# Another table of engine, order, slot and planned time for the 1478 steps of a linear-attention and maxout kernel

## Chip, core and metric

The kernel runs on one NeuronCore of one Trainium2 chip. The metric is device time in microseconds (us) of one launch; a launch takes all inputs from HBM and writes the whole output back to HBM.

## What is computed

The reference is a linear attention with a softmax-like feature map, followed by a maxout feed-forward layer. Its core, shortened:

```python
def phi(x):                                   # q or k: [8, 8, 576, 64], w_phi: [64, 128]
    proj = einsum('bhsd,df->bhsf', x, w_phi)
    proj = proj - max(abs(proj), axis=-1, keepdims=True)
    return concatenate([exp(proj), exp(-proj)], axis=-1)
q_p, k_p = phi(q), phi(k)
kv  = einsum('bhsf,bhsd->bhfd', k_p, v)
num = einsum('bhsf,bhfd->bhsd', q_p, kv)
den = einsum('bhsf,bhf->bhs', q_p, k_p.sum(axis=2))[..., None] + 1e-06
x   = (num / den) with heads side by side     # 4608 tokens x 512
h   = maximum(maximum(x @ w1, x @ w2), x @ w3)  # 768 wide
out = h @ w_out                               # 4608 x 512, float32
```

## The kernel before

**Attention.** The 64 pairs of batch and head are cut into 16 units of four heads (`attention(u)`). Each unit has 18 tiles of 128 rows. A unit goes through these steps, and the letters are the kinds in the code:

- L and Lv load q, k and v. Unit 0 loads q and k in halves as float32 through SyncE's queue (L437) and casts them on VectorE or ScalarE (L444). Units 1 to 3 load q and k through GpSimd's queue with a cast on the way (L451). The later units load float32 through SyncE (L462) and cast on GpSimd (L468). All v loads are SyncE's.
- T transposes q and k, so that the head dimension lies on partitions: on TensorE for units 0 to 3 (L482, with a copy out of PSUM on VectorE at L485), by a transposing DMA on SyncE's queue for the others (L497).
- G projects: for four tiles (or two), one product for q into the bank `psq` and one for k into `psk` (L520). Both have 64 rows of weights, so they use one half of the array's rows each. A unit has five G steps, four of eight products and one of four. Each of them is followed by two reductions of the maximum on VectorE (r, L539) and two exponentials on ScalarE (L533).
- R and V exist from unit 2 on. The q maxima are transposed on TensorE (L547), copied out (mT, L551) and written by a small DMA into a row of the transposed q (V, L555), so that M can subtract the maximum inside the product. Units 0 and 1 subtract it with extra products instead (L601, L604).
- M forms the q projection once more in transposed shape (`psm`, L599), and two exponentials follow on ScalarE (L612).
- v is scaled on GpSimd or VectorE (va, L574), vd fills in the denominator's column (L584), K sums k features times v over 18 tiles (`kvps`, 72 products with 64 rows, L628), N forms numerator and denominator (`psn`, L646), VectorE divides (L652, L653), and X transposes the result into `xT` (on TensorE at L666 for units 0 and 1, by a DMA at L676 for the others).

**Feed-forward.** Nine chunks of 512 tokens (`chunk`) follow the units: eight of one batch each, and one of the 64 last tokens of every batch. w1 was subtracted from w2 and w3 beforehand and w1 @ w_out was formed (L783 transposes w1, L797 multiplies, `pm`). A chunk has 12 up steps of four 128x512 products (`ups`, L699), evacuated by VectorE or ScalarE, and four down tiles: a straight step (L726) and a step over the hidden layer (L731) in one bank `ops`, an evacuation (L739) and a store (L746).

**What sets the order.** Every step is a Node with its engine, its function and its buffers. The string `PLAN` (L96 on) names them in the order in which they are written into the program: the number of the node, the engine (T, D, A, G, S for TensorE, VectorE, ScalarE, GpSimd and SyncE), the slot of each buffer that the step is the first to use, and after the @ a planned time. `plan()` reads it. An engine runs its steps strictly in that order; a step waits for its inputs and for the last users of its slots. The eight PSUM banks are one pool. The planned times only decide one thing more: `fill()` puts idle products (`idler`, L828) into gaps of TensorE's planned times, mostly at the start, so that TensorE keeps running. SyncE, GpSimd and ScalarE also issue DMAs, in the same order as their other steps.

Of the kernel before, what the change touches and what calls it, by code (L numbers as in the profile page):

```python
# [96 lines left out]
0G@0.7 4A@0.7 6S0@0.7 10S0@1.1 2D7@1.1 86G1@1.2 3D@1.5 8S@1.5 13S@2.0 85G@2.0 361S1@2.4 15S0@2.8 1076G@2.9 159G0@3.6 7D2@3.7  # L97
5D@4.2 1G@4.5 158G@5.0 12D@5.1 1079G@5.8 16T5@5.8 17D2@6.5 27T015110@7.3 22T04@7.5 29A@7.8 30D@7.8 28A@8.3 14D@8.6 9A@8.8
26D@9.1 20T5@9.6 31D@9.7 18T6@9.7 24A@9.8 21D@10.3 228G2@10.5 19D@10.5 42T12@10.6 44A@11.0 32T56@11.3 11G@11.3 46D@11.4
1077G@11.4 33A@11.7 35D@11.7 43A@12.2 45D@12.3 23A@12.5 87D3@12.7 25D@12.8 37T31@12.8 88S@12.9 47A1@12.9 93T5@13.0 38A@13.3  # L100
40D@13.4 39A@13.9 94D0@13.9 58T41@14.1 50A0@14.3 41D@14.4 34A@14.5 89T3@14.6 59A@15.0 36D@15.1 55T2@15.2 90D@15.7 61T0@15.8
51A@15.8 60A@16.0 91T3@16.4 63A@16.5 48G@16.9 49D@16.9 67T4@16.9 56A@17.0 64T1@17.3 62A@17.5 68A@17.9 364G1@18.0 115T110601@18.1
69A@18.3 119D@18.5 54A@18.6 66A@18.7 118D@18.8 92D@19.1 53G@19.1 1086T0@19.3 65A@19.3 95T35@19.9 1087A1@20.0 105T71@20.1
52G@20.3 108D@20.6 116A@20.9 109D@21.2 117A@21.3 100T70@21.3 227G@21.4 102A@21.8 103D@21.8 1078G@22.2 57A@22.3 98D@22.4
110T76@22.5 97A@22.8 113D@23.0 162T2@23.1 106A@23.2 101A@23.7 137T30@23.8 163D2@23.8 96A@24.2 166T7@24.2 114D@24.4 164T4@24.5
139A@24.7 1090T2@25.0 167D@25.0 124A1@25.2 165D@25.3 138A@25.4 1088T7@25.5 126G1@25.6 1091A@25.9 70T043@26.0 1089D@26.2
125G@26.7 111A@26.8 140T2@27.2 107A@27.3 104D@27.4 1096T7@27.8 127G@27.8 141A@27.8 72D@28.0 142A@28.2 99D@28.3 112A@28.4
71D@28.9 173T003010@29.1 1097A@29.3 183T56@29.4 73T10@29.6 176D@29.7 174A@29.8 75T4@30.0 187D@30.2 120A@30.3 1094T3@30.4
175A@30.5 121G@30.7 186D@30.8 184A@31.0 160D0@31.4 177D@31.5 185A@31.6 161S@31.7 134T7@31.7 122G@31.8 74D1@32.1 362S1@32.1
79T5@32.2 135A@32.4 128T2@32.5 426S0@32.6 76D0@32.8 1095A@32.9 131T1@33.0 129A@33.4 77T0@33.5 297S0@33.5 80D0@33.5 178T43@33.8  # L110
136A@33.9 1082G@34.0 1098T6@34.1 229D1@34.2 181D@34.3 133A@34.4 182D@34.9 132A@34.9 123A@35.4 168T74@35.5 78D0@35.5 130A@35.6
143T015@35.8 170A@36.1 1080G@36.1 1099D@36.2 180A@36.5 172D@36.8 188T60@36.9 144A@37.2 192D@37.4 145A@37.4 231T2@37.6 191D@37.7
190A@37.8 1092T1@38.1 196A1@38.1 169A@38.3 232D0@38.3 198G0@38.4 189A@38.8 171D@38.9 148T51@39.5 1093A@39.7 152T4@39.8
149D1@40.0 83T0@40.1 199A@40.2 179A@40.4 146T6@40.4 197G@40.5 153D0@40.6 235T2@40.7 84A@40.8 150T1@40.9 236D@41.3 81T5@41.4
147D0@41.5 233T3@41.7 82A@41.9 151D1@42.1 193T6@42.3 154T2@42.4 365G@42.6 194A1@42.7 234D@42.7 242T104701@42.7 155A@43.0
237T10@43.1 195S@43.1 156T6@43.3 245D@43.3 238A@43.6 215T135@43.7 1081G@43.7 296S1@43.8 157D@43.9 243A@44.1 366S1@44.2 241D@44.4
252T24@44.9 246D@45.0 1104T6@45.1 217A@45.1 216A@45.4 255D@45.6 239A@45.7 1112T3@46.1 253A@46.2 240D@46.2 1105A0@46.6 1083D@46.8
247T10@46.9 254A@47.1 257T62@47.3 1110T5@47.4 250D@47.5 1085G@47.8 260D@48.1 203T11@48.4 251D@48.4 1102T6@48.6 1111A@48.6
230S@48.7 256D@49.0 249A@49.1 557S1@49.1 1116T5@49.4 1103A@49.7 1084D@49.9 363S2@50.1 244A@50.2 1114T6@50.3 1117D@50.6 248A@50.7
429G2@50.8 204A@51.1 261D@51.2 209T7@51.2 1124T4@51.4 1113D@51.5 259A@51.6 265A1@51.9 299G0@52.0 258A@52.1 1115D@52.1 262T0@52.3  # L120
1122T5@52.3 205A@52.4 263D0@52.7 210A@52.8 1125D@52.9 264S@53.1 300G@53.1 212T1@53.2 1108T6@53.3 211A@53.4 1123D@53.5 214A@53.9
200T2@54.2 213A@54.3 266G0@54.3 427S0@54.3 367T013010@54.4 1109D@54.4 201A@54.6 387T57@54.7 621S0@54.8 382T14@54.8 371D@55.0
1120T6@55.2 202A@55.2 556S1@55.2 391D@55.6 384A@55.7 385D@55.9 1106T2@56.0 388A@56.2 267G@56.4 383A@56.4 390D@56.5 1121D@56.9
1118T1@56.9 389A@56.9 369A@57.2 370D@57.5 1107A@57.6 377T56@57.8 206T7@58.1 386D@58.1 368A@58.1 1130T2@58.4 208A@58.6 301S2@58.6
380D@58.7 430G@59.1 379A@59.1 224T31@59.3 1119D@59.3 218T0@59.6 207A@59.6 281T50@59.9 225D1@59.9 269T4@60.0 268G@60.2 1131T@60.2
282A@60.2 1101G@60.5 271A@60.5 219D0@60.5 283A@61.0 381D@61.1 270A@61.2 372T57@61.5 624G1@61.7 1132A0@61.8 284T010@61.8
375D@62.1 298S0@62.3 374A@62.4 278T3@62.9 373A@62.9 286D@63.2 220T2@63.2 378A@63.4 376D@63.5 392T4@63.5 1126T0@63.7 279A@63.9
393D1@64.1 221D0@64.3 395A1@64.4 394S@64.5 272T7@64.5 285A@64.6 275T5@64.7 222T4@65.0 273A@65.0 428S3@65.2 287T60@65.3 276A@65.5
# [731 lines left out]
```

## Time and profile before

| | us |
|---|---|
| median of 3 runs (288.76 to 289.62) | 288.84 |
| span of the profiled execution | 287.6 |
| TensorE busy | 275.5 (96%) |
| VectorE, ScalarE, GpSimd busy | 205.7, 198.6, 117.1 |
| idle products (36), busy | 12.0 |
| last product ends | 284.1 |

The span runs from the first to the last instruction of the program; the measured time has 1.2 us more around it. Busy time of TensorE needs care: a record of a 128x512 product is 379 ns long, while the next one starts 216 ns after it, so that records overlap and hide pauses of less than 0.16 us. Starts of successive products are what counts below. Queue times (SPq) are waits of an issuing queue and no work.

### The profile page before, as it was taken

How to read it: one execution, taken by the hardware profiler on the slowest of the kernel's cores; microseconds unless marked ns; L12 is line 12 of the kernel's file. 1: busy time of each engine (PE TensorE's matmuls, PEld its weight loads, DVE VectorE, ACT ScalarE, POOL GpSimd, SP SyncE). 2: the span in 40 equal slices, each digit the busy share in tenths (PEclk: the TensorE clock that was granted, in tenths of full speed). 3: DMA queues.
4: the chain of work that ended last, by engine and by line, in shares of the span. 5: the costliest groups of instructions: out<-in, count | busy, mean ns of one | idle time of the engine just before them, and what ended most of it. 6: DMA issues, size and time to landing. Idle time of an engine off the chain costs nothing.

```text
span 287.6 us, 8596 instructions
## 1 busy us (share of the span) xinstructions
PE 275.5 (96%) x3550; PEld 154.7 (54%) x3590; DVE 205.7 (71%) x434; ACT 198.6 (69%) x460; POOL 117.1 (41%) x100
## 2 busy tenths in 40 slices
PE   8889999999989899999999999999999999999995
PEld 3366675466555455655555466565544654444443
DVE  4679899988979788887879778987863551516511
ACT  1599998999998789895798979997756631040010
POOL 8264688868454349706365434050083000000000
PEclk9999999999999999999999999999999999999999
DMA  7999977999999998999899769787510019410054
GB/s 181 277 248 209 228 298 121 330 282 235 237 176 336 210 260 182 265 267 253 198 238 211 207 122 203 235 171 132 119 41 0 2 41 199 115 34 0 0 153 141
DMA packets 68337, 51.45 MB, mean 179 GB/s; under 512 B 48778, under 2 KB 53066, under 8 KB 68298
## 3 DMA queue, kind: packets, MB, share of 16 engines
q1 hardware_dynamic: 63903, 45.62, 65.6%
q0 software_dynamic: 4000, 4.92, 9.9%
q8 instruction: 28, 0.46, 0.7%
q10 hardware_dynamic: 395, 0.37, 0.4%
q14 instruction: 11, 0.09, 0.1%
HBM read 34.64 MB, written 9.44 MB: 153 GB/s over the span
## 4 chain that ended last, share of the span: by engine, by line
PE 87%; DMA 5%; DVE 3%; ACT 2%; issue 1%; SPq 0%; ACTq 0%; DVEq 0%
PE ups L699 31%; PE ops L731 16%; PE ops L726 10%; PE psn L646 7%; PE kvps L628 6%; PE psq L520 6%; PE psm L599 5%; DMA k_raw<-in_k_dram 3%; DMA qkT<-mT 2%; PE pm L797 2%; DVE mk L539 1%; PE tps L482 1%; DVE mqp L539 1%; ACT Ek L533 1%; ACT Eq L612 1%
## 5 line engine op out<-in xcount | busy, mean ns | idle before, releaser
L699 PE MATMUL ups<-xT,w_bf 128*128 128x512 bf16 x417 | 100.6, 379 | 0.8
L533 ACT ACTIVATE Ek<-psk 128x512 bf16<-128x512 f32 (+1 forms) x160 | 82.0, 572 | 15.3 <-PE psk L520 11.9
L574 POOL TENSOR_TENSOR vab<-v_raw,em 128x1152 bf16<-128x1152 f32 (+1 forms) x35 | 66.8, 1926 | 56.0 <-ACT em L570 45.9
L612 ACT ACTIVATE Eq<-psm 128x512 bf16<-128x512 f32 (+1 forms) x160 | 80.1, 577 | 10.4 <-PE psm L599 9.8
L699 PEld LDWEIGHTS <-w_bf 128*128 128x128 bf16 x432 | 40.2, 98 | 44.4
L539 DVE TENSOR_REDUCE mqp<-psq 128x4 bf16<-128x512 f32 (+1 forms) x80 | 48.5, 633 | 6.4 <-PE psk L520 4.7
L539 DVE TENSOR_REDUCE mk<-psk 128x4 f32<-128x512 f32 (+1 forms) x80 | 49.1, 630 | 5.0 <-PE psk L520 3.3
L731 PE MATMUL ops<-wout_bf,hT 128*128 128x512 bf16 (+2 forms) x219 | 49.8, 367 | 0.6 <-issue 0.3
L705 DVE TENSOR_TENSOR hT<-hT,ups 128x512 bf16<-128x512 bf16 x54 | 35.5, 681 | 16.8 <-PE ups L699 16.3
L739 ACT COPY osb<-ops 128x512 f32<-128x512 f32 (+2 forms) x18 | 10.0, 563 | 36.5 <-PE ops L731 28.9
L707 ACT ACTIVATE hT<-ups 128x512 bf16<-128x512 f32 x38 | 22.4, 612 | 15.5 <-PE ups L699 14.0
L731 PEld LDWEIGHTS <-hT 128*128 128x128 bf16 x228 | 21.1, 98 | 22.2
L653 DVE TENSOR_TENSOR x_sb<-psn,rden 128x320 bf16<-128x320 f32 x64 | 31.5, 492 | 2.2
L646 PEld LDWEIGHTS <-Eq 128*128 128x128 bf16 x640 | 25.9, 98 | 9.7
L739 DVE COPY osb<-ops 128x512 f32<-128x512 f32 (+1 forms) x20 | 13.4, 668 | 21.8 <-PE ops L731 21.6
L646 PE MATMUL psn<-kv_sb,Eq 128*128 128x65 bf16 x640 | 28.2, 194 | 0.0
L520 PE MATMUL psq<-w,qkT 64*128 64x128 bf16 x288 | 24.6, 217 | 2.2 <-DVE mk L539 0.8
L520 PEld LDWEIGHTS <-qkT 64*128 64x128 bf16 x576 | 16.8, 94 | 15.9 <-issue 11.9
L520 PE MATMUL psk<-w,qkT 64*128 64x128 bf16 x288 | 24.5, 217 | 0.2 <-DVE v_raw L460 0.2
L726 PE MATMUL ops<-xT 128*128 128x512 bf16 x85 | 23.1, 379 | 0.9 <-issue 0.5
L599 PE MATMUL psm<-qkT,wphi_m 128*128 128x512 bf16 (+1 forms) x70 | 22.1, 358 | 1.3 <-DMA qkT<-mT 1.2
L652 DVE RECIPROCAL rden<-psn 128x5 f32<-128x5 f32 x64 | 12.1, 189 | 11.8 <-PE psn L646 11.2
(74 smaller groups left out, 237.2 us busy)
## 6 DMA issues: line engine op xcount, KB each, us to landing
v_raw<-in_v_dram SPq DMA_DIRECT2D x16, 576.0 KB
out_dram<-osb SPq DMA_DIRECT2D x65, 128.0 KB
q_raw<-in_q_dram SPq DMA_DIRECT2D x12, 576.0 KB
k_raw<-in_k_dram SPq DMA_DIRECT2D x12, 576.0 KB
w_bf<-in_moe_w_dram POOLq DMA_DIRECT2D x3, 768.0 KB, 15.5
qk_bf<-in_k_dram POOLq DMA_DIRECT2D x3, 288.0 KB, 16.5
qk_bf<-in_q_dram POOLq DMA_DIRECT2D x3, 288.0 KB, 11.6
wout_bf<-in_moe_w_out_dram POOLq DMA_DIRECT2D x1, 768.0 KB, 20.7
```

Source lines behind the costliest of these rows:

```text
L520: nc.tensor.matmul(ps()[:, i, :], lhsT=cols[r, :], rhs=w2[r, c, :], start=True, stop=True)
L533: nc.scalar.activation(Ek[s]()[:, tiles_of(t0, n), :], of(1), EXP, scale=1.0 - 2.0 * s)
L539: nc.vector.tensor_reduce((mq, mk)[c]()[:, tiles_of(t0, n)], of(c), AXX, ALU.max, apply_absolute_value=True)
L574: (nc.vector if n_.eng == "DVE" else nc.gpsimd).tensor_tensor(vab()[:, g, t0:t1, 0:D], vb()[:, t0:t1, :], em()[:, g, t0:t1].unsqueeze(2).t ...
L599: nc.tensor.matmul(psm()[:, 0:w], lhsT=wphi_m, rhs=rhs, start=True, stop=True)
L612: nc.scalar.activation(Eqb()[s][:, cols], psm()[:, 0:w], EXP, scale=1.0 - 2.0 * s)
L646: nc.tensor.matmul(psn()[:, c, :], lhsT=Eqb()[g][:, t0:t0 + P], rhs=kv()[:, pr, ab, g, :], start=(g == 0), stop=(g == 1))
L653: nc.vector.tensor_tensor(x_sb()[:, pr, :, ab, :], psn()[:, :, 0:D], rden().to_broadcast([P, 5, D]), ALU.mult)
L699: nc.tensor.matmul(ups(), lhsT=w_bf[i + 1][:, ct, j * P:(j + 1) * P], rhs=tokens_of(ct), start=(ct == 0), stop=(ct == CT - 1))
L705: nc.vector.tensor_tensor(hT()[:, j, :], hT()[:, j, :], ups(), ALU.max)
L726: nc.tensor.matmul(ops_()[:, 0:width], lhsT=tile_of(ct, tt), rhs=line_w[c_i > MOVE][:, ct, cols], start=(ct == 0), stop=False)
L731: nc.tensor.matmul(ops_()[:, 0:width], lhsT=hT()[:, j, tt * P:(tt + 1) * P], rhs=wout_bf[:, j, cols], start=False, stop=(j == JT - 1))
```

## The change

The program's functions are untouched: the number of every matmul, reduction, exponential and transfer stays. Only the string `PLAN` is another, and it has 13 lines more, so that every line number after it grows by 13 (the products of G are L520 before and L533 now). Its first lines:

```diff
-0G@0.7 4A@0.7 6S0@0.7 10S0@1.1 2D7@1.1 86G1@1.2 3D@1.5 8S@1.5 13S@2.0 85G@2.0 361S1@2.4 15S0@2.8 1076G@2.9 159G0@3.6 7D2@3.7
+2D0@0.70 4A@0.70 10S0@0.70 3D@0.90 6S0@1.18 8S@1.66 13S@2.14 15S0@2.62 11G@3.72 12A0@3.72 0G@3.87 1G@4.42 7D@4.79 86G1@4.92
```

95 of the 1478 steps change their engine (mostly evacuations, between ScalarE and VectorE), and nearly all change their place. All 461 steps of TensorE remain, with 21 idle products where 36 were.

**GpSimd at the start of the program.** Before, the identity was built first and the loads of unit 1 (`qk_bf`), the weights and unit 2 were issued at once:

```order
masks.py:197 MEMSET ident 128x128
masks.py:199 ISA
masks.py:199 AFFINE_SELECT ident<-ident 128x128
L451 DMA qk_bf<-in_k_dram 128x2x576
L451 DMA qk_bf<-in_q_dram 128x2x576
L409 DMA w_bf<-in_moe_w_dram 128x4x768
L451 DMA qk_bf<-in_k_dram 128x2x576
L399 TENSOR_SCALAR minus<-ident 128x128
L451 DMA qk_bf<-in_q_dram 128x2x576
L409 DMA wout_bf<-in_moe_w_out_dram 128x6x512
L451 DMA qk_bf<-in_k_dram 128x2x576
L441 COPY gated<-k_raw 1x1
```

Now the copy `gated`, which waits for the first half of unit 0's k, stands ahead of them all:

```order
L454 COPY gated<-k_raw 1x1
masks.py:197 MEMSET ident 128x128
masks.py:199 ISA
masks.py:199 AFFINE_SELECT ident<-ident 128x128
L412 TENSOR_SCALAR minus<-ident 128x128
L464 DMA qk_bf<-in_k_dram 128x2x576
L464 DMA qk_bf<-in_q_dram 128x2x576
L422 DMA w_bf<-in_moe_w_dram 128x4x768
L464 DMA qk_bf<-in_q_dram 128x2x576
L464 DMA qk_bf<-in_k_dram 128x2x576
L422 DMA wout_bf<-in_moe_w_out_dram 128x6x512
L464 DMA qk_bf<-in_k_dram 128x2x576
```

So GpSimd's first load is issued only after a part of unit 0's data has landed; the two loads of unit 3 come one after the other now, and the weights w2 follow. On SyncE's queue k's first half goes ahead of q's, and the q load of unit 5, which stood ahead of unit 0's v, goes behind unit 1's v.

**TensorE in the last unit's projections.** The names carry buffer numbers here. Before, the G steps of unit 15 follow on one another; this is the end of one (`psk_4764`) and the beginning of the next (`psq_4774`):

```order
L520 LDWEIGHTS qkT_4348
L520 MATMUL psq_4762<-w2_73,qkT_4348 128x128
L520 LDWEIGHTS qkT_4348
L520 MATMUL psk_4764<-w2_73,qkT_4348 128x128
L520 LDWEIGHTS qkT_4348
L520 MATMUL psq_4774<-w2_73,qkT_4348 128x128
L520 LDWEIGHTS qkT_4348
L520 MATMUL psk_4776<-w2_73,qkT_4348 128x128
```

Now the same step of unit 15 ends in front of a down tile's products, which use all 128 rows:

```order
L533 LDWEIGHTS qkT_4578
L533 MATMUL psq_4822<-w2_73,qkT_4578 128x128
L533 LDWEIGHTS qkT_4578
L533 MATMUL psk_4824<-w2_73,qkT_4578 128x128
L739 LDWEIGHTS xT_85
L739 MATMUL ops_4833<-xT_85 128x512
```

This is the rule for all units. G and K have 64 rows of weights in use per product; the transposes of q and k have 128x64; every other product has 128x128. Counted along TensorE's order with idle products left out, the shape of the array's use changes 93 times before and 165 times now. The G and K steps stood in 40 stretches before (9 of a single step, 31 of two to four) and stand in 78 now (62 of a single step, 14 of two, 2 of three).

**VectorE at the same place.** Before, the eight large reductions of unit 15 (`mqp`, `mk`) were a block:

```order
L539 TENSOR_REDUCE mqp0_79<-psq_4762 128x4
L539 TENSOR_REDUCE mqp0_79<-psq_4784 128x4
L539 TENSOR_REDUCE mqp0_79<-psq_4795 128x4
L539 TENSOR_REDUCE mk_4631<-psk_4786 128x4
L539 TENSOR_REDUCE mqp0_79<-psq_4774 128x4
L539 TENSOR_REDUCE mk_4631<-psk_4776 128x4
L539 TENSOR_REDUCE mk_4631<-psk_4764 128x4
L539 TENSOR_REDUCE mk_4631<-psk_4797 128x4
```

Now they are spread among the maxima of the chunk's hidden layer (`hT`) and the divisions:

```order
L552 TENSOR_REDUCE mqp1_80<-psq_4656 128x4
L718 TENSOR_TENSOR hT_4594<-hT_4594,ups_4634 128x512
L718 TENSOR_TENSOR hT_4594<-hT_4594,ups_4683 128x512
L718 TENSOR_TENSOR hT_4594<-hT_4594,ups_4669 128x512
L718 TENSOR_TENSOR hT_4594<-hT_4594,ups_4696 128x512
L665 RECIPROCAL rden_4741<-psn_4723 128x5
L666 TENSOR_TENSOR x_sb_4743<-psn_4723,rden_4741 128x5x64
L552 TENSOR_REDUCE mqp1_80<-psq_4713 128x4
L665 RECIPROCAL rden_4778<-psn_4760 128x5
L666 TENSOR_TENSOR x_sb_4743<-psn_4760,rden_4778 128x5x64
L552 TENSOR_REDUCE mk_4793<-psk_4715 128x4
```

The evacuations of one projection no longer come in a burst; a bank is given back after one or two other steps instead of after up to seven reductions.

Two more moves are spoken of below. The first K of unit 0 stands behind 28 TensorE steps before and behind 25 now: one transposing step of four products (unit 2), one G step of four (unit 1) and one M step (unit 1) that stood ahead of it stand behind it. And in several units fewer TensorE steps lie between R and the first M, which is the time that the copy mT and the small DMA V have. For unit 3 these were 15 steps (six up steps, one straight step, three M, three G and two N of other units); now they are seven (one M, one N, two G, and three steps of down tiles).

More of the change, by code (lines that the diff above doesn't have):

```diff
@@ L101 @@
[L101 to L126, printed above, removed]
```

257 lines of the change are left out of this document (148 added, 109 removed).

## The prediction

> **What bounds the kernel now.** I read the page first (busy shares, chain), then TensorE in four stages, its waits, and single starts in the timeline. From the page:
>
> ```profile
> span 287.6 us, 8596 instructions
> PE 275.5 (96%) x3550; PEld 154.7 (54%) x3590; DVE 205.7 (71%) x434; ACT 198.6 (69%) x460; POOL 117.1 (41%) x100
> PE 87%; DMA 5%; DVE 3%; ACT 2%; issue 1%; SPq 0%; ACTq 0%; DVEq 0%
> GB/s 181 277 248 209 228 298 121 330 282 235 237 176 336 210 260 182 265 267 253 198 238 211 207 122 203 235 171 132 119 41 0 2 41 199 115 34 0 0 153 141
> ```
>
> TensorE holds 87% of the chain that ended last. Where it is not fully busy shows in the stages (window, its length, then PE, PEld, DVE, ACT and POOL busy) and in TensorE's waits (sum, times, longest):
>
> ```profile
> 0.00:27.10 27.10, 23.26 (x289) 12.69 (x290) 18.70 (x45) 17.24 (x41) 13.89 (x23) 1.00 1.04 230
> 27.10:82.00 54.90, 54.27 (x932) 33.12 (x943) 49.74 (x108) 52.32 (x124) 39.96 (x30) 1.00 1.02 242
> 82.00:96.00 14.00, 11.92 (x186) 6.81 (x181) 12.49 (x27) 11.63 (x28) 7.74 (x6) 1.00 0.97 247
> 96.00:284.10 188.10, 186.02 (x2159) 102.05 (x2185) 124.72 (x256) 117.13 (x269) 55.55 (x43) 1.00 0.64 149
> ...
> PE psm L599 <- DMA qkT<-mT: 1.2, 1, 1.2
> ...
> PE psq L520 <- DVE mk L539: 0.8, 1, 0.8
> ```
>
> After 27 us TensorE pauses only between 82 and 96 us. The first stage looks 86% busy, but idle products fill it. So I count TensorE's time from what products cost back to back. Pieces of the chain (start, length) give the rates:
>
> ```profile
> 24.31 0.57 PE tps L482 x16
> ...
> 27.11 1.50 PE kvps L628 x72
> ...
> 36.85 1.09 PE kvps L628 x72
> ...
> 40.02 0.63 PE psn L646 x20
> ...
> 49.05 2.59 PE ups L699 x12
> ...
> 281.46 2.63 PE ops L731 x24
> ```
>
> A 128x512 product takes 2.59/12 = 0.216. The program has 870 of them (432 up, 350 down, 64 M, 24 `pm`): 187.7 us. 16 K at 1.09 make 17.4, 64 N at 0.63/2 20.0. The 80 G steps make 16.1 by the pair steps of 0.056 below (64 of 0.224, 16 of 0.112). The remainder (12 transposing steps, narrow products of M and of the last tile, extra products of units 0 and 1) makes 13.3 at like rates. **Work: 254.5 us.** It doesn't change. The last product ends at 281.46 + 2.63 = 284.1, so 29.6 us are something else.
>
> A part of these is the price of changing the array's shape:
>
> ```profile
> 90.04 1.89 PE L699 MATMUL ups<-xT,w_bf 128*128 128x512 bf16 x8
> 91.86 0.23 PE L520 MATMUL psq<-w,qkT 64*128 64x128 bf16 x1
> ...
> 92.04 0.22 PE L520 MATMUL psk<-w,qkT 64*128 64x128 bf16 x1
> 92.09 0.22 PE L520 MATMUL psq<-w,qkT 64*128 64x128 bf16 x1
> ...
> 92.49 0.22 PE L520 MATMUL psk<-w,qkT 64*128 64x128 bf16 x1
> 92.64 1.04 PE L699 MATMUL ups<-xT,w_bf 128*128 128x512 bf16 x4
> 93.51 1.03 PE L726 MATMUL ops<-xT 128*128 128x512 bf16 x4
> ```
>
> From `ups` to `ops`, same shape, four products take 93.51 - 92.64 = 0.87 = 4 x 0.216. From 90.04 to the first `psq` eight take 1.82, 0.096 more than 8 x 0.216. From 92.49 to `ups` it is 0.15 instead of a pair step of about 0.055, again 0.096 more. From one G step to the next (92.04 to 92.09) nothing is added. So **a change of shape costs 0.096 us**, and the order has 93 before: 8.9 us. The remaining 29.6 - 8.9 = 20.7 us are waits:
>
> - ahead of the first K (first `kvps` at 27.1): the 28 steps ahead of it are 8.8 us of work with 17 changes (1.6), so 16.7 of waits;
> - 82 to 96 us: 14.00 - 11.92 = 2.1;
> - scattered: the other 1.9.
>
> **The change, part by part.** *Changes of shape.* 165 against 93, 72 more at 0.096: **+6.9 us**. Ahead of the first K there are 16 instead of 17; all the added ones stand behind it, where TensorE has hardly any idle time that could absorb them (54.27 busy of 54.90, 186.02 of 188.10). [...]
>
> *The start.* These rows set it now (start, length; in brackets the idle time before and its releaser):
>
> ```profile
> 1.43 0.91 POOL L451 DMA_DIRECT2D qk_bf<-in_k_dram  x1
> 3.75 0.46 DVE L444 CAST qk_bf<-q_raw 128x576 bf16<-128x576 f32 x1 [1.76 <-DMA q_raw<-in_q_dram]
> 6.49 0.69 DVE L485 COPY qkT<-tps 128x1024 bf16<-128x1024 bf16 x1 [0.94 <-PE tps L482]
> 8.68 0.67 ACT L444 CAST qk_bf<-q_raw 128x576 bf16<-128x576 f32 x1
> 9.86 0.46 DVE L444 CAST qk_bf<-k_raw 128x576 bf16<-128x576 f32 x1 [1.50 <-DMA k_raw<-in_k_dram]
> 10.37 0.69 PE L482 MATMUL tps<-ident,qk_bf 128*64 128x128 bf16 x17 [0.67 <-DVE qk_bf L444]
> 15.58 1.29 DVE L539 TENSOR_REDUCE mk<-psk 128x4 f32<-128x512 f32 x2 [0.15 <-ACT Ek L533]
> 16.46 1.15 POOL L574 TENSOR_TENSOR vab<-v_raw,em 128x576 bf16<-128x576 f32 x1 [3.26 <-DMA v_raw<-in_v_dram]
> 19.34 2.26 POOL L574 TENSOR_TENSOR vab<-v_raw,em 128x576 bf16<-128x576 f32 x2
> ```
>
> Unit 0's second k half is awaited until 9.86 and its v until 16.46, because GpSimd's loads share the engines from 1.43 on. In the change these are issued after about 5 us (the gate waits for a first half, as the cast at 3.75 does; identity and `minus` take 1.3 more). Unit 0's 1.77 MB then move alone: at the 277 GB/s of the second slice 6.4 us, so from about 2.3 to 8.7, the second k half at about 6.6. Cast on ScalarE (0.67) 7.3, its transposes (10.37 before) at about 7.5, their copy (0.69) done by 8.8. VectorE then has eight large reductions and two small ones, with three copies between: 8 x 0.63 (half of 1.29, less an overlap) + 2 x 0.35 + 1.5 = 7.2, from 7.5 to 14.7. The four va of unit 0, all on GpSimd now, start at about 14.6 (the last maxima they need, then `em`) and take 4 x 1.13 = 4.5; with a weight load's issue (0.8) and two vd (0.5) the last is done at 20.4. v has long landed; unit 1's loads need to be there by 11. So the first K starts at about 21.0, with 8.2 us of work and 1.5 of changes ahead of it: 11.3 of waits instead of 16.7, **-5.4**. Bounds: 20 (VectorE denser than these rows) to 24 (see the rival).
>
> *82 to 96 us.* What caused these two pauses:
>
> ```profile
> 84.08 0.23 PE L520 MATMUL psq<-w,qkT 64*128 64x128 bf16 x1 [0.78 <-DVE mk L539]
> ...
> 88.91 6.78 DMA qkT<-mT
> ```
>
> The first is a G step that wants a bank which VectorE still has to reduce, after G steps in a burst; the spread steps of the change take the burst away. The second is a V whose DMA took 6.78 us behind other transfers of SyncE's queue. In the change unit 6 has 9.1 us of TensorE work between R and M instead of 7.3. Both go: **-2.1**.
>
> *New waits.* TensorE's work between R and M shrinks for units 3, 4, 5, 7 and 13 from 5.2 to 13.0 us to between 3.5 and 4.1, with the changes in it 3.7 to 4.4. Unit 15 before has 3.7 and pauses nowhere, so this is just enough where V's queue is empty. Bounds: 0, and 1.2 (the one wait above) for each of five, 6.0; I take 0.8 in all, near the row of unit 15. The 1.9 scattered stay. Engine changes of evacuations cost nothing: VectorE (49.74 of 54.90) and ScalarE (52.32) are the fullest where the next stage is TensorE's, and their sums move by under 2 us. The idle products that go were filling waits. The end of the program, with the same last tile and stores, stays 3.5 us.
>
> Sum: +6.9 - 5.4 - 2.1 + 0.8 = +0.2. **Forecast: span 287.6 + 0.2 = 287.8; with the 1.2 us that the runs' median has around the span, 289.0 us**, no change that a measurement tells apart (0.3%, 0.9 us, is about its limit here).
>
> **Rivals.**
>
> *Changes of shape are free* (faster), because other waits would fill the same time. Then a spread order costs nothing and the gains remain: -5.4 - 2.1 + 0.8 = -6.7, 282.1 us. For it: the pauses at 84 us lie among G steps. Against it: from 96 us on TensorE is busy 186.02 of 188.10, and the rows show 0.096 between products that wait for nothing. Half of it, 285.5, would need 35 changes in other waits.
>
> *The start doesn't come forward* (slower). GpSimd's first load now starts 3.5 us later, and this queue holds unit 1's q and k, both weights and units 2 and 3 in one line:
>
> ```profile
> qk_bf<-in_k_dram POOLq DMA_DIRECT2D x3, 288.0 KB, 16.5
> ...
> wout_bf<-in_moe_w_out_dram POOLq DMA_DIRECT2D x1, 768.0 KB, 20.7
> ```
>
> TensorE's order has unit 1's transposes ahead of the first M of unit 0. If these loads keep their pace of before, 3.5 us later, everything behind waits: the first K at 24, +3.0, 292.1 us. It decides from a landing of unit 1's k and q later than about 12 us. For it: 16.5 us from issue to landing. Against: they no longer share with unit 0's.
>
> *Small transfers late* (slower). Two V, or transposing DMAs, come behind loads as the one at 88.91 did: 2 x 1.2 and a missed bank, +3.0 in place of 0.8, 291.3 us. It decides where less than about 3.5 us of work lie behind an R, or a load stands just ahead.
>
> **How the numbers follow.** Forecast 0.64 (faster by over 0.3% 0.14, within 0.32, slower 0.18: its terms are uncertain by 1 to 1.5 us), free changes 0.10 (faster), late start 0.13 and late transfers 0.13 (both slower). Faster 0.24, same 0.32, slower 0.44. The forecast's own range is 287.3 to 290.9. The range that leaves out the free changes' lower half and the worst of the late cases is 286.6 to 292.0.
>
> **What would show it.** Right: first `kvps` at 20.5 to 21.5; `psq` behind a 512-wide product always 0.31 after it; no wait of TensorE on `mk` near 84; from 30 us on scarcely any pause, and yet TensorE some 7 us behind in the same work by the end. Wrong: a first `kvps` after 23; TensorE waiting for `qkT<-mT`, `qkT<-qk_bf` or `qk_bf`; a start-to-start of 0.22 across changes of shape.

## The result and the profile after

The changed kernel takes **293.81 us** in the median of four runs (293.46 to 295.33) beside 289.23 for the kernel before on the same chip (288.76 to 289.70): ratio 1.0162, 95% interval 1.0130 to 1.0195. It is slower by 4.6 us, where the forecast was no change (289.0, range 286.6 to 292.0). The profiled execution has a span of 291.7 us, 4.1 more than before. (In every run here the time is about 1.8 us more than the span of the same execution; the 1.2 us named ahead compare a median with the span of another execution.)

From the page of the changed kernel (span, busy times, the clock by slice, the chain by engine):

```profile
span 291.7 us, 8546 instructions
PE 280.7 (96%) x3534; PEld 153.1 (53%) x3575; DVE 208.2 (71%) x439; ACT 198.3 (68%) x451; POOL 119.0 (41%) x104
...
PEclk9999889999999999999999999999999999999999
...
PE 84%; DMA 10%; POOL 1%; issue 1%; DVE 1%; SPq 0%; ACT 0%; POOLq 0%
```

TensorE is busy for 5.2 us more with the same work, and the chain has twice as much DMA in it (10% instead of 5%). The clock's row shows two slices (29 to 44 us) below 9. By stages (window, length, then busy time of PE, PEld, DVE, ACT and POOL, the granted clock, the share of the transfer engines and GB/s):

```profile
0.00:21.20 21.20, 18.05 (x256) 10.67 (x256) 14.87 (x37) 15.04 (x30) 13.86 (x24) 1.00 1.03 210
21.20:56.00 34.80, 32.28 (x530) 20.09 (x535) 28.99 (x62) 27.16 (x65) 21.38 (x17) 0.95 1.03 272
56.00:82.00 26.00, 25.74 (x407) 14.46 (x405) 24.20 (x52) 22.95 (x54) 14.65 (x12) 1.00 0.89 198
82.00:96.00 14.00, 13.89 (x203) 7.63 (x203) 10.92 (x23) 11.84 (x31) 11.14 (x10) 1.00 0.89 255
96.00:288.60 192.60, 190.75 (x2160) 100.30 (x2185) 129.22 (x267) 121.07 (x273) 57.97 (x44) 1.00 0.63 148
```

Two terms of the forecast can be read at once: the first K is there (next rows) and the stage from 82 to 96 us has no pause left (13.89 of 14.00; before 11.92). The surprise is the second row: between the first K and 56 us TensorE lacks 2.5 us, the clock is below 1, and the transfer engines are fully taken on the average (1.03, though only 0.49 from 36 to 39 us). The rows of TensorE in that stage (start, length; in brackets the idle time before and its releaser):

```profile
21.23 0.20 PE L641 MATMUL kvps<-vab,Ek 64*128 64x65 bf16 x1
...
33.43 0.21 PE L641 MATMUL kvps<-vab,Ek 64*128 64x65 bf16 x2 [0.91 <-POOL vab L587]
34.54 2.08 PE L641 MATMUL kvps<-vab,Ek 64*128 64x65 bf16 x70 [0.90 <-POOL vab L587]
...
36.97 1.22 PE L679 MATMUL pxT<-ident,x_sb 128*128 128x128 bf16 x10
```

The first `kvps` starts at 21.23 (forecast 21.0). Unit 1's K then waits for GpSimd's va twice, 1.81 us, and runs at half speed: 70 products take 2.08, where before all 72 took 1.09. What the va wait for stands on SyncE and on GpSimd:

```profile
21.48 0.37 SPq L475 DMA_DIRECT2D v_raw<-in_v_dram  x1
```

```profile
30.00 4.49 POOL L587 TENSOR_TENSOR vab<-v_raw,em 128x576 bf16<-128x576 f32 x4 [9.20 <-DMA v_raw<-in_v_dram]
```

Unit 1's v is issued at 21.48 (14.06 before) and its first user starts at 30.00. What its issue waits for stands in the chain:

```profile
7.88 11.52 DMA qk_bf<-in_k_dram
...
19.44 0.65 PE tps L495 x15
...
21.41 0.05 DVE v_raw L473
```

The load of v has a gate, a copy on VectorE (L473), which now stands behind the copy of unit 2's transposed k; that k is issued at 7.88 and lands at 19.40. The table itself plans the load of v (its node 88) at 12.9 us before and at 21.06 now.

To compare kernels with different numbers of changes of shape I use one measure in the rest: the **time lost** up to a step, which is its start less TensorE's work ahead of it (at the rates of the prediction) less 0.096 us per change of shape. For the two kernels:

| | first K | first N of unit 1 | near 56 us | last step |
|---|---|---|---|---|
| before: time lost | 16.6 | 17.0 | 17.2 | 20.4 |
| changed: time lost | 11.5 | 16.0 | 16.5 | 18.0 |

So 5.1 us were gained at the first K and 4.4 of them were gone by 56 us. From there on the changed kernel loses 1.5 and the one before 3.2, which keeps 1.7 of the 2.1 forecast. With 72 x 0.096 = 6.9 for the shapes: 6.9 - 0.7 - 1.7 = +4.5, which is the later start of the last step (288.08 instead of 283.58). The part behind it is 0.4 shorter, so the span grows by 4.1.

### The profile page after: what moved, and what is told of

It is laid out like the page before. It is cut to its first block, busy times and chain, and to the rows that moved or that the text cites. A ratio compares the mean times of both kernels' runs of the same rounds, so it can differ in the third digit from the quotient of the medians.

```text
span 291.7 us, 8546 instructions
## 1 busy us (share of the span) xinstructions
PE 280.7 (96%) x3534; PEld 153.1 (53%) x3575; DVE 208.2 (71%) x439; ACT 198.3 (68%) x451; POOL 119.0 (41%) x104
## 4 chain that ended last, share of the span: by engine, by line
PE 84%; DMA 10%; POOL 1%; issue 1%; DVE 1%; SPq 0%; ACT 0%; POOLq 0%
PE ups L712 31%; PE ops L744 16%; PE ops L739 10%; PE psn L659 7%; PE kvps L641 6%; PE psq L533 6%; PE psm L612 5%; DMA qk_bf<-in_k_dram 4%; DMA v_raw<-in_v_dram 3%; DMA qkT<-mT 2%; DMA k_raw<-in_k_dram 2%; POOL vab L587 1%; PE pxT L679 1%; PE tps L495 0%; SPq L450 0%
## 5 line engine op out<-in xcount | busy, mean ns | idle before, releaser
L712 PE MATMUL ups<-xT,w_bf 128*128 128x512 bf16 x414 | 101.7, 380 | 0.9
L587 POOL TENSOR_TENSOR vab<-v_raw,em 128x1152 bf16<-128x1152 f32 (+1 forms) x36 | 68.0, 1906 | 74.0 <-ACT em L583 40.5
L625 ACT ACTIVATE Eq<-psm 128x512 bf16<-128x512 f32 (+1 forms) x160 | 81.2, 575 | 13.0 <-PE psm L612 11.9
L552 DVE TENSOR_REDUCE mqp<-psq 128x4 bf16<-128x512 f32 (+1 forms) x80 | 49.7, 633 | 10.1 <-PE psk L533 9.2
L720 ACT ACTIVATE hT<-ups 128x512 bf16<-128x512 f32 x32 | 19.1, 604 | 23.5 <-PE ups L712 23.3
L533 PEld LDWEIGHTS <-qkT 64*128 64x128 bf16 x576 | 16.6, 95 | 24.4 <-issue 19.2
L533 PE MATMUL psq<-w,qkT 64*128 64x128 bf16 x288 | 28.4, 220 | 0.8 <-DVE qkT L498 0.4
L752 ACT COPY osb<-ops 128x512 f32<-128x512 f32 (+2 forms) x25 | 14.3, 583 | 21.2 <-PE ops L744 20.0
L533 PE MATMUL psk<-w,qkT 64*128 64x128 bf16 x288 | 28.3, 220 | 0.0
L722 DVE TENSOR_SCALAR hT<-ups 128x512 bf16<-128x512 f32 x22 | 14.9, 684 | 13.8 <-PE ups L712 13.8
L641 PE MATMUL kvps<-vab,Ek 64*128 64x65 bf16 x1152 | 21.5, 193 | 1.8 <-POOL vab L587 1.8
## 6 DMA issues: line engine op xcount, KB each, us to landing
qk_bf<-in_k_dram POOLq DMA_DIRECT2D x3, 288.0 KB, 11.5
```

The source lines that it names most:

```text
L533: nc.tensor.matmul(ps()[:, i, :], lhsT=cols[r, :], rhs=w2[r, c, :], start=True, stop=True)
L552: nc.vector.tensor_reduce((mq, mk)[c]()[:, tiles_of(t0, n)], of(c), AXX, ALU.max, apply_absolute_value=True)
L587: (nc.vector if n_.eng == "DVE" else nc.gpsimd).tensor_tensor(vab()[:, g, t0:t1, 0:D], vb()[:, t0:t1, :], em()[:, g, t0:t1].unsqueeze(2).t ...
L625: nc.scalar.activation(Eqb()[s][:, cols], psm()[:, 0:w], EXP, scale=1.0 - 2.0 * s)
L641: nc.tensor.matmul(kvps[ab]()[:, t // NT, g, :], lhsT=Ek[g]()[r, t, :], rhs=vab()[r, g, t, :], start=(t + g == 0), stop=(t == UT - 1 and g ...
L712: nc.tensor.matmul(ups(), lhsT=w_bf[i + 1][:, ct, j * P:(j + 1) * P], rhs=tokens_of(ct), start=(ct == 0), stop=(ct == CT - 1))
```

## The experiments

Theory after the result: unit 1's v is late, TensorE's wait for it lets the clock fall, and both together eat the start's gain. Rivals: the fall has another cause; and (put on record with E7) the sum of the transfers bounds the first 50 us, so that any wait that is removed comes back elsewhere. Where only words of the table are moved, a diff shows these words. Ratios are against the kernel before, run beside it.

### Unit 1's v earlier (E1)

```diff
-87D1@20.81 88S@21.06
+87D1@12.55 88S@12.58
```

Unit 5's two loads, which follow on SyncE, got a gate of their own where the old one stood.

> The changed kernel; only the load of unit 1's v goes out earlier: its gate stands on VectorE behind unit 0's seventh reduction of k instead of one unit later, so that v is issued near 13.5 us instead of 21.48 and lands near 22. (The two loads of unit 5 that stand behind it on SyncE keep their time of issue by a gate of their own where the old one stood.) Theory, late v: TensorE's two waits of 0.91 and 0.90 us on va ahead of unit 1's K go, and with them the fall of the granted clock to 0.5 at 34.61; 1.8 + 2.2 = 4 us less, a span of 287.7 (291.7 in the changed kernel), the same time as before within 0.5%. Rival, small steps: the clock falls because TensorE runs transposes, G steps and N steps there instead of wide products, whatever it waits for; then only the waits go, 1.8 us at most, a span of 289.9 or more, and 0.5 stands in the clock's rows near 34 us as it does now.

Measured: span 291.0, ratio 1.0133 [1.0086, 1.0179]. v went out at 12.89 and landed 7.6 us later, unit 1's K no longer waits, and the clock is 1.0 from end to end. Yet 0.7 us are gained, not 4. TensorE's waits (sum, times, longest):

```profile
PE tps L495 <- DMA qk_bf<-in_k_dram: 1.5, 1, 1.5
...
PE tps L495 <- DMA qk_bf<-in_q_dram: 1.0, 1, 1.0
PE pwT L796 <- DMA w_bf<-in_moe_w_dram: 0.9, 1, 0.9
```

These are three transfers that GpSimd had issued earlier. The wait for q, unit 1's, ended at 12.37, before v went out, and comes in E16 without any change to v (1.6); so the earlier v can only have made the other two late, unit 2's k (wait until 21.58) and the weights (until 17.24). Neither the theory's 287.7 nor the rival on small steps fits (the clock does not fall); the rival on the sum of the transfers fits these two waits.

### Idle products in the wait (E2, E5, E13)

Eight products go ahead of unit 1's K, in E2 in one bank, in E13 in two (E5: six in two):

```diff
     spans, todo, free = {}, [(n.start, n.fn) for n in order], 0.0
+    k1 = [n for n in order if n.kind == "K"][1]
+    for i in range(8):
+        todo.append((k1.start - 0.001, make(3 + i % 2)))
```

> The changed kernel with eight idle products of 128x512 (0.216 us each, 1.73 in all) directly ahead of unit 1's K, in the bank that K is to use; v lands as late as in the changed kernel and va ends at 34.5 as there. Theory, an idle array lowers the clock: the wait stays but is filled, the clock stays 1.0, unit 1's K takes 1.09 us instead of 2.08 and the steps behind it their usual times; 2.0 to 2.6 us less, a span of 289.1 to 289.7. Rival, small steps or something that runs by the time since the start: 0.5 again near 34.6 us, a span of 291.5 to 292.

> The changed kernel with six idle products ahead of unit 1's K, alternately in the two banks that K is to use. (In the run with eight in one bank, each waited for the end of the one ahead in its bank and took 0.43 instead of 0.216, 3.41 us in all, so that they outlasted the wait on va; the clock stayed 1.0.) Theory, an idle array lowers the clock: with 1.3 to 1.5 us of products from about 33.1 on the wait for va is filled and not outlasted, unit 1's K takes about 1.1 us instead of 2.08, and unit 1's first N starts near 37.0 instead of 38.0; a span of 290.2 to 290.8 (291.7 in the changed kernel). Rival, the fall is set by the time since the start: 0.5 near 34.6 again and a span of 291.5 or more.

> The changed kernel with eight idle products ahead of unit 1's K, alternately in the two banks that K is to use; the run with six told nothing on the clock, since its profiled execution shows a mean clock of 0.949 from end to end. Theory, a mostly idle stretch of 3.41 us lowers the clock for the next 3.41: eight products of 0.216 us last from about 33.1 to 34.9, K runs at full speed right behind them (1.1 us instead of 2.08) and unit 1's first N starts near 37.3 instead of 38.0: a span of 290.7 to 291.2, clock 1.0 from start to end. Rival: a fall to 0.5 near 34 to 38 us all the same, a span of 292 or more.

Measured: E2 span 292.6, ratio 1.0204 [1.0146, 1.0263]; E13 span 293.4, ratio 1.0189 [1.0151, 1.0226]. E5 has ratio 1.0181 [1.0130, 1.0232], and its profiled execution tells nothing, because it ran at a mean clock of 0.949 throughout. E2's rows:

```profile
33.10 3.41 PE L844 MATMUL idler<-idle 128*128 128x512 bf16 x8
36.56 1.27 PE L644 MATMUL kvps<-vab,Ek 64*128 64x65 bf16 x72
```

and E13's:

```profile
33.94 1.89 PE L844 MATMUL idler<-idle 128*128 128x512 bf16 x8
35.76 1.56 PE L644 MATMUL kvps<-vab,Ek 64*128 64x65 bf16 x72
37.47 0.73 PE L682 MATMUL pxT<-ident,x_sb 128*128 128x128 bf16 x10
```

In one bank the eight start every 0.43 us, (3.41 - 0.38)/7 with 0.38 for a single record, so that each starts only after the one ahead has ended; in two they start every 0.22, (1.89 - 0.38)/7, with records that overlap. Behind the filled wait the clock stays 1.0 in both, which fits the theory that an idle array lowers it (the last section has more on this). But neither is faster: in E2 the products outlast the wait, and E13's execution lost 2 us more ahead of the first K, where TensorE waited 1.4 us for unit 1's q (until 12.95) and the clock was 0.5 from 13.15 to 16.56. **The fall of the clock is real, but a run without it isn't faster.**

### The price of a change of shape (E3, E9, E10)

E3 is the kernel before with 24 wide products moved between adjacent G steps, 48 changes more. Two of the 24:

```diff
-1110T5@47.4
+1110T5@47.1
-1120T6@55.2
+1120T6@54.55
```

> The kernel before, with 24 places behind 45 us where a product of 128x512 is moved by one step to stand between two adjacent G steps: 141 changes of the array's shape instead of 93, with all else (instructions, engines, slots, idle products, every other queue) as before. Theory, a change costs 0.096 us: 48 x 0.096 = 4.6 us more, a span of 292.2 (287.6 before), ratio 1.016. Rival, changes are hidden in waits that would come anyway: less than 1.5 us more, ratio under 1.005.

Measured: span 298.0, ratio 1.033 [1.0277, 1.0383], +10.4 us, more than the price (4.6). New waits of TensorE are a part of the other 5.8: behind 45 us the profile names 4.8 us of waits, beside 2.8 in the kernel before; where the remainder lies is open. Two of the waits:

```profile
PE ups L699 <- DVE mqp L539: 1.0, 2, 0.8
PE ops L726 <- DVE mqp L539: 0.8, 1, 0.8
```

A G step that comes 0.9 us later holds its reduction, and behind this, in VectorE's fixed order, the evacuations that free the banks of `ups` and `ops`. So E3 refutes "hidden", but it doesn't give the price by itself. E9 and E10 do: 45 small products in the last 50 us, where the other engines are mostly idle (VectorE 15.62 busy, ScalarE 5.49 and GpSimd 0.40 of the 41.50 us from 237 to 278.5 in the kernel before), with all 128 rows of the array (E9, `make(i, 128)`) or with 64 (E10, shown).

```diff
+        if n.eng == "PE" and 237.0 < n.start < 278.5:
...
+            todo.append((t, make(i, 64)))
...
+                nc.tensor.matmul(idler[:, 0:64], lhsT=idle[0:rows, :], rhs=idle[0:rows, 0:64], start=True, stop=True)
```

> The kernel before with 45 small extra products (64 columns, all 128 rows of the array, the shape of their neighbours) set singly between up and down steps from 237 to 278 us, where TensorE alone sets the time. It is the measure for the next kernel: 45 x about 0.03 us (a product of 65 columns takes 0.313/10) up to 45 x 0.1, so a span of 289 to 292 (287.6 before).

> As the last, but the 45 small products use 64 of the 128 rows, the shape of the G steps: 90 changes of shape more, and nothing else different. Theory, a change costs 0.096 us by itself: 90 x 0.096 = 8.6 us more than the kernel with 45 products of the same shape. Rival, the pause belongs to G steps (their operands, their banks) and not to the shape: within 1.5 us of it.

E9 (same shape), ratio 1.0043 [1.0018, 1.0068]:

```profile
249.81 0.19 PE L834 MATMUL idler<-idle 128*128 128x64 bf16 x1
249.84 1.03 PE L704 MATMUL ups<-xT,w_bf 128*128 128x512 bf16 x4
250.70 0.19 PE L834 MATMUL idler<-idle 128*128 128x64 bf16 x1
```

E10 (other shape), ratio 1.0386 [1.0356, 1.0417]:

```profile
249.89 0.20 PE L834 MATMUL idler<-idle 64*128 64x64 bf16 x1
250.02 1.04 PE L704 MATMUL ups<-xT,w_bf 128*128 128x512 bf16 x4
250.99 0.20 PE L834 MATMUL idler<-idle 64*128 64x64 bf16 x1
```

From one small product to the next it is 0.89 us with the same shape and 1.10 with the other: 0.21 for two changes, **0.105 each**. The medians say the same: 300.48 - 290.87 = 9.6 us for 90, 0.107 each. (The spans, 290.9 and 297.8, differ by less, because E9's profiled execution has a wait of 2.8 us at 83 us and a fall of the clock behind it, 0.50 from 85.92 to 89.33.) The shape alone costs this, with no G step in it.

### The gate at the start (E4)

```diff
-11G@3.72
+11G@11.4
```

> The changed kernel with GpSimd's gate (the copy that waits for unit 0's first half of k) moved back behind the loads of units 1 to 3, so that these go out from about 1.4 us on, beside unit 0's, as in the kernel before. Theory, the start's gain comes from this gate: unit 0's second k half comes near 10 us and its v near 16 again, the first kvps at 25 to 27 instead of 21.2, and the end 3 to 5 us later (295 to 297 us span), less what the later waits on unit 1's v give back. Rival, the gain comes from the order on VectorE and GpSimd: first kvps below 23, span within 1.5 us of 291.7.

Measured: span 291.7, ratio 1.0142 [1.0093, 1.0191]. The first `kvps` comes at 23.16, 1.9 later than in the changed kernel's first trace and 3.9 earlier than before. That does not measure the gate, because this execution's clock fell ahead of the first K:

```profile
11.40:14.82 3.42, 3.42 (x39) 1.57 (x33) 3.19 (x7) 2.62 (x6) 1.97 (x4) 0.50 1.16 209
```

And with the gate in place, in the same order up to there, the first `kvps` came at 21.2 to 23.2 (the changed kernel, E2, E6, E16, E13). What the gate moves is seen earlier: unit 0's second half of k is cast at 9.05 here, at 7.58 in the changed kernel and at 9.86 before. Its share in the gain at the first K stays open. At the end nothing differs (medians 293.37 and 293.81). Unit 1's K waits as in the changed kernel:

```profile
34.94 0.21 PE L641 MATMUL kvps<-vab,Ek 64*128 64x65 bf16 x2 [0.87 <-POOL vab L587]
36.05 1.24 PE L641 MATMUL kvps<-vab,Ek 64*128 64x65 bf16 x70 [0.90 <-POOL vab L587]
```

The same two waits, and yet 70 products take 1.24 here instead of 2.08: the clock did not fall there. This is taken up in the last section.

### v in the middle, and the weights later (E7, E14)

E7 issues v at 18.20, when unit 2's loads are nearly in, and moves the first wm step behind one N and one G step:

```diff
-87D1@20.81 88S@21.06 1098T2@23.14
+87D1@16.9 88S@16.95 1098T2@24.9
```

> The changed kernel with unit 1's v issued near 17.5 us, after the loads of unit 2 are nearly in (21.48 in the changed kernel, 12.89 in the run with the early v), so that it shares only with wout and unit 3's loads, which are needed later; TensorE's first wm step, which needs wout, moves behind one N and one G step. Theory, each transfer early enough for its first user: v lands near 24, va of unit 1 runs from about 26.9 to 31.4, the waits of 0.91 and 0.90 and the clock's fall go, wout comes up to 1.4 us later and costs at most 0.7: 2.9 to 3.6 us less, a span of 288.1 to 288.8. Rival, the first 33 us are bound by the sum of the transfers: what v gains others lose, as in the run with the early v, a span above 290.5.

Measured: span 290.6, ratio 1.0111 [1.0062, 1.0161], clock 1.0. K's waits are gone, and 2.3 us are gained at unit 1's first N. Ahead of that, the G step that now stands in front of wm waits for VectorE's reduction until 25.32 (first row); the first `pm` follows at 25.67, without a wait of its own, `wout` having landed at 25.3. Behind the first N, V is waited for (second row):

```profile
PE psk L533 <- DVE mqp L552: 1.1, 1, 1.1
...
PE psm L612 <- DMA qkT<-mT: 0.6, 1, 0.6
```

1.1 us are left at the end: the rival's side of 290.5 by a hair. `wout` did land later than in the changed kernel (there at 23.2), as the rival says. But wm no longer waited for it; the wait came at the G step, which in the changed kernel stands behind wm and starts at 25.36 without one.

E14 leaves v where it was and moves two loads of weights behind unit 1's va:

```diff
-1077G@11.62 1078G@19.46
+1077G@30.5 1078G@30.52
```

> The changed kernel with GpSimd's loads of the second and third weight matrix (w_bf, 768 KB each, issued at 10.99 and 19.71) moved behind its four va of unit 1; unit 1's v is issued where it was, at 21.5. Theory, v came late because it shared the transfer engines with these loads: now it shares only the end of unit 3's, lands near 26 instead of 29.86, va runs from 26.7 to 31.2, TensorE's waits of 0.91 and 0.90 us and the clock's fall go, 3.6 us less at unit 1's first N (34.5 instead of 38.0). The weights come at about 36 and 40; GpSimd's differences of weights, from 38.5 on in the changed kernel, are as early as before: a span of 288.1 to 288.8. Rival, the weights' lateness is passed on to the first up steps (43 us): TensorE waits there for GpSimd's differences, and the span is 290.5 or more.

Measured: span 292.2, ratio 1.0199 [1.0164, 1.0235]. v lands 6.4 us after its issue instead of 8.4, so it did share with the weights; K starts at 32.46 without a wait, and at unit 1's first N the lost time is 12.5, so that the start's gain is still there. At the first up step 2.1 of it are gone, by 56 us all. TensorE and GpSimd:

```profile
41.45 1.90 PE L712 MATMUL ups<-xT,w_bf 128*128 128x512 bf16 x8 [2.06 <-DVE mk L552]
```

```profile
39.28 6.28 POOL L782 TENSOR_TENSOR w_bf<-w_bf 128x1024 bf16<-128x1024 bf16 x3 [3.08 <-DMA w_bf<-in_moe_w_dram]
```

The profile names a reduction of VectorE, which was long done; what ends at 41.4 is the first of GpSimd's three differences of weights, which waited 3.08 us for the load. The rival's case, but the transfer engines were not full: from 30 to 33 us their share is 0.01. GpSimd, which issues these loads, was busy with va:

```profile
32.39 1.57 POOL L422 DMA_DIRECT2D w_bf<-in_moe_w_dram  x2
```

The weights were late because they were issued late. An issue from another engine as soon as v has landed (27.9) was not tried.

Lost time in all these variants of the changed kernel:

| | first K | first N of unit 1 | near 56 us | last step |
|---|---|---|---|---|
| E1, v at 12.9 | 13.7 | 14.8 | 15.6 | 17.4 |
| E7, v at 18.2 | 11.8 | 13.7 | 15.4 | 16.9 |
| E14, weights late | 11.5 | 12.5 | 16.6 | 18.5 |
| E13, idle products | 13.5 | 16.1 | 17.6 | 19.8 |
| E4, gate late | 13.4 | 16.0 | 16.5 | 18.0 |
| E16, unchanged | 12.9 | 15.7 | 16.5 | 18.9 |

Whatever is moved, 15.4 to 17.6 us are lost by 56 us (17.2 in the kernel before). But at unit 1's first N the variants differ, and by v. Where its load is placed as in the changed kernel and shares with the same loads, unit 1's K can go on only 12.8 to 13.1 us after v's issue (from 21.48 to 34.54 in the first trace, from 22.86 to 35.71 in E16, from 23.29 to 36.05 in E4), and this N starts at 37.7 to 38.0; in the first trace, where v was earliest, the slow clock took the difference. Where v comes earlier, the N starts at 34.5 (E14), 35.7 (E7) and 36.8 (E1).

### The changed kernel once more (E16)

> The changed kernel once more, unchanged, to see what its waits ahead of unit 1's K and the clock do in another execution. Theory, windows of 3.41 us counted from the first clock record: the waits of 0.9 and 0.9 us come again (v lands near 29.9), and the clock falls to 0.5 only if the window that holds both is less than about half busy, so not in every execution. Rival: no such waits, or a fall at the same 34.6 us whatever the windows' start.

Measured: span 292.6, ratio 1.0126 [1.0083, 1.0169]. In this execution the first `kvps` is at 22.61, K waits 0.25 and 0.90, and the clock doesn't fall. Other waits stand in the place; the first, for unit 1's q, ends at 12.98, ahead of the first K, and is most of the 1.4 us by which that came later:

```profile
PE tps L495 <- DMA qk_bf<-in_q_dram: 1.6, 1, 1.6
PE psm L612 <- DMA qkT<-mT: 1.2, 2, 0.7
...
PE kvps L641 <- POOL vab L587: 0.9, 1, 0.9
```

Without the fall it is no faster. Of the ten executions of the changed kernel (four with the result, six here), the five with a mean clock of at least 0.999 have spans of 290.6 to 292.6 us, the others 291.7 to 293.7. So the slow clock of the first trace is not the cause. The late v is common to both traces: K goes on 13.1 us after v's issue in the first and 12.9 in this one (34.54 - 21.48 and 35.71 - 22.86).

### Fewer changes of shape, and the pauses alone (E6, E8, E11, E12, E15)

E6 has another order behind 44 us with 127 changes instead of 165, worked out from fixed durations of the steps; E8 is E6 with E7's start. E11 (138 changes, on E7) and E12 (101, on the kernel before) move only steps of TensorE, VectorE and ScalarE, though many of them, and some further than the expectation says. One of E11's places on TensorE, where two G steps (582 and 502) come together:

```diff
-582T56@94.51 1178T4@94.63 502T003100@95.50
+582T56@94.63 502T003100@94.88 1178T4@95.23
```

> The changed kernel with another order behind 44 us (planned time): G steps moved beside one another, and their evacuations moved along with them on VectorE and ScalarE, so that 127 changes of the array's shape are left of 165; engines, slots and all that stands ahead of 44 us as in the changed kernel. Theory, a change costs 0.096 us and moving the evacuations along avoids the waits that the split kernel got: 38 x 0.096 = 3.6 us less, a span of 288.1. Rival, regrouping brings back waits on banks as at 84 us in the kernel before (0.8 each): less than 1.5 us gained, a span above 290.2.

> The two last together: unit 1's v near 17.5 us and the regrouped order behind 44 us. If both theories hold, 3.6 + 3.2 = 6.8 us less than the changed kernel: a span of 284.9, 0.9% faster than the kernel before. If one of them fails, 288 to 289.

> The kernel with unit 1's v near 17.5 us (span 290.6), and behind 44 us an order with 138 instead of 165 changes of shape, made by moving only steps of TensorE, VectorE and ScalarE, most of them by one or two places; SyncE's and GpSimd's orders stay. (The regrouped kernel had moved SyncE's transposing loads too, and waited 8.5 us for three of them.) Theory: 27 x 0.096 = 2.6 us less, a span of 288.0. Rival, G steps that stand together wait for banks and their reductions hold up other evacuations: 290 or more.

> The kernel before with steps of TensorE, VectorE and ScalarE behind 44 us moved by a few places, so that V's data and the banks at 82 to 96 us come earlier than they are wanted; 101 instead of 93 changes of shape; engines, slots, idle products and SyncE's order as before. Theory: the pauses of 2.1 us go, 8 x 0.096 = 0.8 come, a span of 286.3 (287.6 before), 0.4% faster than the kernel before. Rival, the pauses come from the transfers' traffic and appear at other places: 287.6 or more.

Measured: ratios 1.0825 [1.0755, 1.0895], 1.0784 [1.0727, 1.0841], 1.0454 [1.0411, 1.0498] and 1.0462 [1.0425, 1.0499]; spans 313.4, 313.0, 300.8 and 301.8. All four theories were wrong, by 12.8 to 28 us. In E6 a transposing load is the worst:

```profile
PE psq L533 <- DMA qkT<-qk_bf: 8.5, 3, 4.9
```

In E12, where SyncE's order is that of before, it is many small waits for evacuations, behind 45 us among others:

```profile
PE ups L699 <- ACT Ek L533: 1.0, 2, 0.7
PE psk L520 <- DVE mqp L539: 1.0, 1, 1.0
PE psm L599 <- DVE mk L539: 0.8, 1, 0.8
```

Orders from fixed durations don't hold here. That fewer changes of shape can be had without such waits is therefore not shown. E15 moves two steps of the kernel before, at its pauses between 82 and 96 us:

```diff
-459S@87.4
+459A@89.95
-1146T7@83.3
+1146T7@82.95
```

> The kernel before with two single steps moved, both at the pauses between 82 and 96 us: unit 6's V goes out on ScalarE's queue (behind six of unit 4's Eq) instead of SyncE's, where loads and stores stand ahead of it, and one up step goes ahead of unit 8's first G step, which waits for a bank. 95 changes of shape instead of 93. Theory: the waits of 1.2 and 0.8 us go, 2 x 0.1 come, a span of 285.8 (287.6 before), ratio 0.994. Rival, the evacuations set the pace in this stage (ScalarE is held 0.7 us longer by the issue): 287 or more.

Measured: span 287.2, ratio 0.9979 [0.9946, 1.0011], which can't be told from no change. The bank's wait is gone, V's is not:

```profile
89.41 1.32 ACTq L555 DMA_DIRECT2D qkT<-mT  x1
```

```profile
95.17 0.60 PE L599 MATMUL psm<-qkT,wphi_m 128*128 128x512 bf16 x2 [1.25 <-DMA qkT<-mT]
```

On ScalarE's queue V went out at 89.41 (88.91 before) and took 5.71 us instead of 6.78, so that it still came only at 95.1. Its place on SyncE's queue is thus at most a small part of the lateness; that the loads and stores running beside it (the transfer engines' share is 0.97 from 82 to 96 us in the kernel before) make the rest is the author's guess, and not tried. No version here beats the kernel before.

## Why the prediction was wrong, by its own steps

- **Changes of shape, +6.9: right.** 72 more, at 0.096 in the rows and 0.105 by themselves (E10); nothing hid them. The rival "free" is refuted by E3 and E10.
- **The start, -5.4: right at its place.** The first `kvps` came at 21.23 (forecast 21.0, bounds 20 to 24), and at 22.61 in a second execution; where the start is that of the kernel before, it came at 26.0 to 27.8 (six executions: before, E3, E9, E10, E12, E15). That it is the gate that brings this is not shown (E4). And the step took a gain at the first K for a gain at the end. "Unit 1's loads need to be there by 11" looked at q and k and never asked when unit 1's v comes.
- **82 to 96 us, -2.1: right** (13.89 of 14.00 busy). Over the whole part behind 56 us it is 1.7. In the second execution (E16) it is 0.8. That V was held up by other transfers of SyncE's own queue is not borne out: on ScalarE's it took 5.71 us instead of 6.78 (E15).
- **New waits, +0.8: this is the step that failed.** It looked only at V and mT between R and M, from unit 3 on, and there, in the first trace, it was right: TensorE never waits for V (in E16 it does, 1.2 us in two waits). The new waits came between the first K and 56 us, where the lost time grows by 5.0 us instead of 0.6: 4.4, mis-sized by 3.6 (in E16 3.0 instead of 0.8). The wait that it left out is that of unit 1's K for v, whose load stands 7.4 us later than before, behind unit 2's k. Where it does, K goes on 12.8 to 13.1 us after this load's issue in three traces, and with v earlier (E1, E7, E14) unit 1's first N comes 1.3 to 3.6 us earlier than in the first trace: this much is shown. Why the gain is lost again by 56 us when v comes earlier stays open. The waits that the traces name up to there have different causes: in E1 other loads behind v's issue, in E7 a reduction of VectorE and a V, in E14 weights issued late while the transfer engines stood idle, and a V. That loads delay one another fits E1's k and E7's `wout`. That their sum bounds this stage is not shown, and E14 speaks against it; no run had fewer bytes.
- **The end, unchanged at 3.5:** 3.1.
- **Engine changes of evacuations, nothing:** not tried by themselves. Behind 56 us, where 76 of the 95 lie, the changed kernel loses less than the one before (1.5 and 3.2), so nothing shows there.
- Of the rivals, "the start doesn't come forward" has 292.1, near the result, but by luck: its 3.0 us were to show at the first K. Its mechanism came in part. Unit 1's q, which was to decide at about 12 us, let TensorE go on at 12.03 in the first trace (0.33 us of wait) and at 12.98 in E16 (1.6 us). "Small transfers late" did not come in the first trace. "From 30 us on scarcely any pause", which was to show the forecast right, failed at 33.43.
- Two figures of the working are 0.1 too high (289.0 + 3.0 = 292.0; 289.0 + 2.2 = 291.2). Nothing hangs on it.

## What to carry to other kernels

A gain at an early step counts only when each later step that waits for a transfer has been followed to its own transfer, and that to what its issue waits for. When a load is moved, ask what it makes late, and on which engine its issue has to wait. The price of a change of the array's shape came out nearly the same in two measures here (0.096 us in the rows of the kernel before, 0.105 in E10, so 0.2 for a step set alone among others), but grouping such steps moves their evacuations, and where VectorE and ScalarE are nearly full (49.74 and 52.32 of 54.90 us from 27 to 82 us in the kernel before) this cost more than it saved in every order tried (spans of 300.8 to 313.4 in E6, E8 and E11, of 290.6 and 291.7 without it). One trace's chain names one way of losing time; a second execution of the same kernel (E16) lost as much with other waits, and a difference of 1.9 us at an early step (E4) was no more than executions with the same start differ by.

## What the runs showed of the hardware

**The clock fell by windows of 3.41 us.** In the changed kernel's trace the first full-speed record of the clock starts at 3.89 us, and the granted clock changes at 34.61, 38.02 and 290.61, which is 9, 10 and 84 times 3.413 us later. In the kernel before it starts at 5.72 and changes at 289.03, 83 times 3.413 us later. The falls inside the programs follow windows in which TensorE is less busy. The changed kernel, the window with both waits and the one behind it:

```profile
31.20:34.61 3.41, 1.59 (x40) 1.31 (x38) 2.24 (x7) 2.10 (x6) 3.41 (x4) 1.00 1.11 281
34.61:38.02 3.41, 3.41 (x89) 3.21 (x89) 0.97 (x2) 0.95 (x3) 1.60 (x2) 0.50 0.88 187
```

E4, whose windows lie so that the same two waits fall into two of them:

```profile
31.88:35.29 3.41, 2.39 (x51) 1.92 (x50) 2.98 (x8) 2.96 (x8) 3.41 (x4) 1.00 1.11 284
35.29:38.70 3.41, 2.65 (x111) 2.55 (x110) 1.30 (x3) 1.40 (x4) 2.28 (x3) 1.00 0.47 140
```

1.59 of 3.41 us busy (47%) is followed by 0.5; 2.39 (70%) is not. Other windows that are followed by 0.5 are 0.63 busy (18%, E9, 82.51 to 85.92) and 1.45 (43%, E4, 7.99 to 11.40); others that are not are 2.16 (63%, the kernel before, 94.47 to 97.88), 2.19 (64%, the changed kernel, 7.30 to 10.72) and 2.26 (66%, E16, 32.71 to 36.12). Elsewhere in the traces, the ends of the programs left out, falls follow 12 to 59% and none follows 60% or more, but seven windows between 46 and 58% had none: between 46 and 60% the busy share of these traces doesn't settle it, and some records are missing (the page of the changed kernel has 414 products and 432 weight loads of `ups`). From the end of the second wait to unit 1's first N the changed kernel took 3.48 us (34.54 to 38.02), E4 1.96 (36.05 to 38.01): the same two waits, 0.91 and 0.90 us in one and 0.87 and 0.90 in the other, cost 1.5 us more or nothing, by where they fall.

**Two streams shared the transfer engines.** v's 576 KB took 8.4 us from issue to landing beside GpSimd's loads of weights and 6.4 without them (E14). In those 8.4 us (21.48 to 29.86 in the changed kernel) the queue of GpSimd's loads (q0) moved 1.26 MB and SyncE's (q1) 0.78.

**Idle products in one bank took double.** Eight in a row in one bank start every 0.43 us (3.41 in all, E2), in two banks every 0.22 (1.89 in all, E13).
